# Half of the first k tile brought in uncast over SyncE's queue and cast on ScalarE, with new engine orders, in a fused attention and MLP kernel

## The chip, the cores and the metric

The kernel runs on one core of a Trainium2 chip. The metric is the device time of one execution in microseconds, the median of the runs shown. A profile of one execution of its own lies beside the runs.

## The reference

Two stages, the second of which eats what the first gives:

```
q, k, v: [8, 8, 576, 64]   beacon_k, beacon_v: [8, 8, 16, 64]      (batch, head, token, dim; float32)
k_all = concat(beacon_k, k);  v_all = concat(beacon_v, v)           592 keys
a = softmax(q k_all^T / 8), causal on the 576 tokens, the 16 beacon keys seen by all
x = (a v_all), heads side by side                                   [4608, 512]
h = x w_in;  g = h * sigmoid(1.702 h);  out = g w_out               [512, 2048], [2048, 512]
```

## The kernel before, in words

**Tiles and stages.** The 64 heads are worked in 16 sets of four (two sets to a batch). A set's q and k each come from HBM as one tile of 128 partitions by 1152 elements (18 tokens by 64 dims to a partition, `e_load_qk`, L415). The load is a DMA issued by POOL, and it casts float32 to float16 on its way. DVE turns each tile (`e_turn`, L464) by 32x32 transposes into `qT` and `kT`. TensorE makes the scores of a set in chunks (`e_qk`, L492): QK chunk 0 is the first half of the queries of set 0, chunk 1 that of set 1, chunks 2 to 4 the second half of set 0, chunks 5 to 7 that of set 1. ScalarE takes the exponentials (L517), DVE or POOL cuts them at the causal diagonal (L531, L538), TensorE multiplies by v (`e_av`, L597; with x = 2 it makes the softmax sums by a product with ones instead), DVE inverts the sums (`e_z1`, `e_z2`) and normalizes into `xT` (L631). From there the MLP runs in groups of tokens: group 0 is tokens 0 to 255, group 1 the next 256, later ones 512 tokens each. The first product is at L655 (`m1`), its gate in groups 0 and 1 is a tanh on ScalarE (L669) and a multiply on DVE (L688), the second product is at L700 and, for later groups, L769 (`m2`).

**PSUM.** Score chunks use one buffer `s` of four banks, so a new chunk waits until the exponential of the one before has read it. A ring of four more banks `u` serves everything else: AV products, m1 tiles, and the four heads of QK chunks 1 and 2 (`RINGED = (1, 2)`). A ring bank is free again when its reader is done: the exponential, the normalization, the z transpose, the gate.

**Order of the work.** The program makes a list of operations (`plan.op`) with what they depend on. Each gets a number in the order of its making. `ORDER` (L16) holds, written out for each engine, the numbers in the order in which that engine issues them. So each engine works strictly in that order, and an instruction that waits holds all behind it. DMAs issued by POOL (lists "POOL" and "Q") have eight in flight at most (`LANES`): the ninth issue waits on POOL until the first of them has landed. `lat` (L233) holds the delays with which the order was made.

**The start.** SP and ACT load the beacon keys of set 0 (`load_bk(0, 1, ...)`, four small DMAs), SP those of set 1 (four more). POOL issues q of set 0, k of set 0, k of set 1, q of set 1, then v and w_in in pieces: v of batch 0 in six (the beacon values and five blocks of keys, called v0 to v4 here), w_in in eight (four column quarters c0 to c3 by two row halves of 256 KB in float16 each). The orders of the first work, by names that stand for the numbers:

```
POOL q0 k0 k1 q1 | v0 w(c1) w(c0) v4 w(c0) beacon v, v2 v1 w(c2), keep masks, w(c1) | mask, q2 k3 v3 w(c2) ...
DVE  beacon cast, q0 turn, k0 turn, set 1's cast and two turns, masks, z and norms of the first halves,
     ..., three gates, ... k2 turn ...
PE   qk0 qk3 qk1 qk4 qk2 qk5 | AV sums of sets 0, 1; AV 1.1 | qk6 | AV 0.0, sums of set 0's second half,
     AV 0.1, AV 1.0 | qk7 | m1 (four of group 0), five AVs of the second halves, m1 (four), ...
ACT  exp 0, 0, 3, four of 1, 4, two of 2, 5, two of 2, 6, 7, then tanh
```

"AV 1.0" is the product of set 1 with the first of two interleaved halves of v. PE fills its early waits with dummy products on `scrap` (L1377), so that a busy PE before 16 us is not all work.

Of the kernel before, what the change touches and what calls it, by code (L numbers as in the profile page):

```python
# [8 lines left out]
F32 = mybir.dt.float32  # L9
# [8 lines left out]
        76, 119, 100, 101, 102, 103, 111, 122, 112, 113, 114, 140, 126, 149, 154, 142, 129, 133, 131, 152, 145, 163,  # L18
        166, 169, 172, 136, 138, 156, 161, 159, 175, 178, 184, 181, 199, 238, 205, 202, 217, 243, 208, 193, 245, 211,
        214, 248, 194, 220, 269, 187, 188, 223, 274, 195, 189, 276, 224, 196, 279, 190, 225, 411, 252, 283, 259, 255,  # L20
        226, 414, 229, 230, 231, 257, 417, 290, 288, 264, 262, 293, 286, 295, 424, 232, 323, 315, 311, 313, 301, 319,
        305, 307, 309, 303, 321, 317, 331, 327, 329, 325, 442, 433, 349, 354, 355, 350, 351, 356, 352, 445, 436, 440,
        438, 357, 360, 471, 376, 361, 362, 370, 363, 577, 371, 365, 372, 377, 366, 580, 481, 367, 373, 378, 368, 586,
        484, 379, 486, 488, 605, 382, 518, 496, 607, 383, 384, 385, 520, 610, 490, 512, 516, 492, 500, 494, 506, 502,
        514, 510, 504, 508, 498, 549, 543, 544, 538, 539, 540, 545, 541, 596, 738, 550, 565, 546, 551, 552, 741, 566,
        567, 568, 601, 744, 619, 599, 603, 554, 555, 751, 626, 624, 556, 557, 622, 769, 559, 560, 561, 562, 628, 772,
        760, 571, 572, 573, 648, 574, 658, 638, 656, 798, 765, 763, 654, 646, 632, 634, 642, 640, 644, 630, 650, 636,
        652, 808, 767, 703, 676, 677, 681, 682, 904, 683, 678, 704, 684, 679, 907, 705, 811, 815, 813, 913, 687, 688,
        697, 689, 690, 932, 706, 698, 692, 693, 699, 934, 694, 695, 700, 839, 937, 923, 709, 710, 711, 829, 821, 712,
        827, 837, 823, 817, 833, 835, 841, 819, 847, 825, 831, 843, 845, 1065, 946, 928, 865, 870, 866, 867, 871,  # L30
        868, 1068, 926, 930, 951, 949, 953, 1071, 876, 877, 878, 872, 873, 1078, 886, 887, 888, 879, 881, 882, 1096,
        883, 892, 893, 884, 894, 1099, 889, 961, 895, 1087, 1125, 898, 899, 900, 901, 969, 965, 957, 955, 967, 959,
        981, 963, 985, 979, 975, 973, 983, 977, 971, 1144, 1135, 1094, 1090, 1003, 1004, 1005, 1014, 1006, 1147,
        1140, 1092, 1142, 1138, 1153, 1008, 1009, 1015, 1019, 1016, 1010, 1172, 1011, 1017, 1020, 1203, 1021, 1174,
        1030, 1022, 1024, 1025, 1026, 1027, 1177, 1031, 1032, 1033, 1207, 1205, 1209, 1219, 1235, 1211, 1036, 1212,
        1037, 1215, 1038, 1039, 1239, 1237, 1163, 1186, 1251, 1223, 1221, 1241, 1243, 1244, 1253, 1225, 1255, 1247,
        1227, 1228, 1257, 1189, 1191, 1193, 1170, 1168, 1166, 1259, 1260, 1231, 1342, 1283, 1288, 1326, 1263, 1289,
        1284, 1328, 1330, 1358, 1290, 1285, 1286, 1360, 1344, 1291, 1362, 1346, 1332, 1294, 1334, 1335, 1295, 1348,
        1351, 1296, 1338, 1304, 1297, 1350, 1299, 1374, 1300, 1301, 1364, 1305, 1302, 1354, 1306, 1378, 1367, 1366,
        1380, 1307, 1382, 1383, 1376, 1310, 1311, 1312, 1316, 1313, 1370, 1386, 1317, 1318, 1319, 1449, 1465, 1406,  # L40
        1411, 1407, 1469, 1408, 1412, 1467, 1451, 1474, 1471, 1473, 1409, 1453, 1481, 1413, 1414, 1417, 1458, 1455,
        1418, 1457, 1427, 1419, 1477, 1420, 1487, 1485, 1483, 1497, 1422, 1423, 1428, 1424, 1490, 1425, 1461, 1489,
        1501, 1433, 1429, 1430, 1503, 1434, 1505, 1435, 1506, 1436, 1439, 1440, 1441, 1442, 1529, 1493, 1530, 1509,
        1499, 1531, 1534, 1550, 1540, 1551, 1532, 1541, 1535, 1542, 1536, 1537, 1552, 1553, 1543, 1545, 1546, 1547,
        1548, 1556, 1557, 1558, 1559, 1562, 1563, 1564, 1565,
    ],
    "ACT": [
        3, 1, 77, 79, 120, 107, 104, 105, 106, 123, 118, 117, 141, 116, 115, 143, 146, 164, 167, 170, 173, 176, 179,
        182, 185, 200, 239, 203, 206, 244, 209, 246, 212, 215, 249, 218, 270, 275, 277, 221, 280, 191, 197, 412, 415,
        227, 418, 425, 427, 233, 324, 314, 316, 302, 320, 308, 312, 306, 310, 322, 318, 304, 332, 328, 330, 326, 443,  # L50
        353, 446, 472, 475, 578, 581, 587, 590, 606, 608, 519, 521, 513, 491, 497, 517, 493, 495, 501, 515, 511, 503,
        507, 505, 509, 499, 611, 542, 739, 742, 745, 754, 752, 770, 773, 629, 649, 659, 639, 657, 799, 655, 635, 633,
        641, 643, 645, 647, 651, 631, 637, 653, 802, 905, 680, 908, 917, 914, 933, 935, 938, 840, 822, 828, 838, 818,
        824, 834, 836, 820, 848, 842, 826, 830, 832, 844, 846, 1066, 869, 1069, 1072, 1079, 1081, 1097, 1100, 1129,
        1126, 962, 966, 958, 970, 960, 956, 964, 968, 982, 986, 976, 974, 980, 984, 978, 972, 1145, 1007, 1148, 1157,
        1154, 1173, 1175, 1204, 1178, 1208, 1210, 1206, 1236, 1214, 1216, 1218, 1220, 1238, 1240, 1252, 1242, 1222,
        1224, 1226, 1254, 1246, 1250, 1248, 1230, 1258, 1256, 1234, 1232, 1343, 1266, 1327, 1264, 1262, 1359, 1329,
        1287, 1331, 1361, 1345, 1347, 1333, 1337, 1339, 1341, 1349, 1357, 1353, 1363, 1375, 1365, 1355, 1379, 1369,
        1373, 1377, 1381, 1385, 1387, 1371, 1389, 1450, 1466, 1470, 1452, 1472, 1468, 1410, 1454, 1476, 1480, 1456,
        1464, 1482, 1478, 1460, 1488, 1486, 1484, 1498, 1462, 1496, 1502, 1504, 1508, 1492, 1512, 1494, 1500, 1510,  # L60
        1533,
    ],
    "DVE": [
        73, 75, 74, 97, 98, 99, 80, 82, 81, 110, 109, 78, 108, 127, 128, 150, 151, 130, 132, 153, 155, 134, 92, 237,
        135, 165, 168, 171, 137, 87, 139, 157, 235, 158, 162, 174, 160, 177, 236, 180, 183, 186, 266, 267, 201, 207,
        204, 268, 210, 213, 216, 421, 408, 219, 409, 410, 222, 468, 297, 253, 254, 260, 423, 422, 261, 284, 256, 258,
        285, 291, 289, 265, 263, 292, 287, 294, 296, 300, 469, 470, 298, 299, 429, 430, 431, 337, 338, 341, 583, 333,
        334, 432, 342, 343, 335, 345, 434, 344, 339, 435, 336, 340, 346, 347, 437, 441, 439, 358, 348, 477, 585, 478,
        479, 480, 364, 584, 482, 483, 735, 369, 748, 485, 374, 487, 489, 380, 386, 750, 749, 737, 736, 615, 592, 522,
        523, 593, 534, 535, 536, 594, 795, 530, 526, 537, 531, 527, 528, 532, 595, 529, 533, 597, 598, 524, 525, 547,  # L70
        553, 616, 617, 618, 602, 620, 600, 621, 604, 627, 756, 625, 623, 757, 558, 758, 759, 563, 910, 569, 796, 761,
        797, 762, 575, 766, 764, 804, 912, 805, 911, 1075, 806, 807, 660, 661, 672, 668, 768, 809, 669, 662, 810,
        670, 673, 664, 663, 671, 665, 685, 674, 816, 812, 666, 667, 814, 919, 675, 920, 691, 921, 696, 922, 701, 924,
        1062, 707, 1077, 1063, 942, 925, 713, 1076, 1064, 943, 1195, 1150, 857, 944, 858, 849, 945, 1122, 850, 859,
        851, 947, 929, 853, 854, 948, 852, 861, 855, 862, 927, 931, 952, 856, 860, 954, 863, 864, 950, 1083, 874,
        1124, 1123, 1084, 1085, 880, 885, 1086, 890, 1196, 1088, 896, 902, 1131, 1089, 1152, 1132, 1133, 987, 988,
        989, 1151, 1197, 991, 992, 1134, 990, 1198, 1136, 999, 1095, 1137, 995, 996, 1000, 1091, 1141, 1093, 997,
        1139, 993, 1199, 1001, 1143, 998, 994, 1200, 1201, 1002, 1012, 1018, 1159, 1160, 1202, 1023, 1028, 1182,
        1161, 1034, 1162, 1213, 1183, 1217, 1184, 1185, 1040, 1267, 1164, 1165, 1268, 1187, 1245, 1249, 1188, 1229,
        1233, 1190, 1192, 1194, 1171, 1169, 1167, 1261, 1265, 1322, 1323, 1324, 1271, 1269, 1270, 1325, 1275, 1272,  # L80
# [42 lines left out]
class Plan:  # L123
# [109 lines left out]
    def lat(self, d, o):  # L233
        if o.eng == "Q":
            return 300 if d.eng == "SP" else 1200
        if d.name == "bk" and d.eng != "DVE":
            return {"bk0": 2500, "bk1": 5200}.get(o.name, 9000)
# [7 lines left out]
def kernel(  # L245
# [11 lines left out]
    nc = tc.nc  # L257
# [202 lines left out]
    def f32(ap):  # L460
        return ap.bitcast(F32)
# [952 lines left out]
```

## Time and profile before

| what | us |
|---|---|
| runs | 322.94, 323.44, 324.39 (median 323.44) |
| the profiled execution | 323.13 |
| its span | 321.4 |
| PE busy | 310.9 (97%) |
| DVE busy | 245.7 (76%) |
| ACT busy | 219.9 (68%) |
| POOL busy | 112.7 (35%) |
| QK chunk 0 starts on PE | 8.93 |
| first m1 matmul | 22.21 |
| last matmul ends | 317.6 |

The span is the time from the first to the last instruction of the program; 1.7 us of the execution lie around it. Busy shares are averages over the span. Where a row of the timeline gives "[idle before <-releaser]", it is the time the engine stood still ahead of this instruction and what ended the wait. The landing of a DMA is its issue time plus the microseconds that the DMA view gives it.

### The profile page before, as it was taken

The numbers are of one execution on the slowest core, as the hardware profiler recorded it, in microseconds if no ns is written. First come the engines' busy times: TensorE is split into PE (matmuls) and PEld (weight loads), VectorE is DVE, ScalarE is ACT, GpSimd is POOL, SyncE is SP. The second block draws the span as 40 slices with busy tenths as digits, with TensorE's granted clock in tenths as the row PEclk, the third lists the DMA queues.
The fourth block names the chain that finished last, engine by engine and source line by source line (L and its number), as shares of the span: only waits on it lengthen the run. The fifth ranks groups of instructions, "written<-read, shape, count | busy, mean of one in ns | idle before, by whom it ended". The sixth has DMA issues, their size and how long they took to land.

```text
span 321.4 us, 10238 instructions
## 1 busy us (share of the span) xinstructions
PE 310.9 (97%) x4465; PEld 230.0 (72%) x4465; DVE 245.7 (76%) x481; ACT 219.9 (68%) x277; POOL 112.7 (35%) x178
## 2 busy tenths in 40 slices
PE   7779999999999999999999999999999999999995
PEld 6557765644886467754778878746888888888884
DVE  3579963997894888976888969888988975684683
ACT  1783778686767787598867685778779786665520
POOL 7777558590226703573083208320320000000000
PEclk9999999999999999999999999999999999999999
DMA  7999999998028961299174707700021000010113
GB/s 120 159 194 206 195 198 179 197 188 104 2 63 115 168 91 35 20 163 122 23 78 88 120 4 71 107 33 2 4 72 61 2 20 17 33 68 34 68 58 107
DMA packets 58222, 28.85 MB, mean 90 GB/s; under 512 B 41280, under 2 KB 53568, under 8 KB 58176
## 3 DMA queue, kind: packets, MB, share of 16 engines
q0 software_dynamic: 47552, 18.49, 49.4%
q1 hardware_dynamic: 10560, 9.69, 9.2%
q8 instruction: 35, 0.57, 0.7%
q14 instruction: 11, 0.09, 0.1%
q10 hardware_dynamic: 64, 0.01, 0.0%
HBM read 37.22 MB, written 9.44 MB: 145 GB/s over the span
## 4 chain that ended last, share of the span: by engine, by line
PE 91%; DMA 3%; POOL 3%; ACT 1%; issue 1%; DVE 0%; POOLq 0%
PE u L769 31%; PE u L655 26%; PE u L856 11%; PE u L597 10%; PE s L506 8%; PE u L700 5%; DMA w<-in_moe_w_in_dram 3%; POOL w L439 1%; ACT E L517 1%; POOL vb L433 1%; POOL kn L417 0%; ACT L676 0%; POOL qn L417 0%; POOL E L538 0%; DVE xT L631 0%
## 5 line engine op out<-in xcount | busy, mean ns | idle before, releaser
L517 ACT ACTIVATE E<-s 128x2048 f16<-128x2048 f32 (+5 forms) x63 | 95.6, 1532 | 41.4 <-PE s L506 37.7
L655 PE MATMUL u<-xT,w 128*128 128x256 f16 (+1 forms) x512 | 87.4, 326 | 0.7 <-issue 0.5
L538 POOL TENSOR_SCALAR_AFFINE_SELECT E<-E 128x512 f16<-128x512 f16 (+3 forms) x78 | 48.1, 634 | 91.4 <-ACT E L517 91.3
L655 PEld LDWEIGHTS <-w 128*128 128x128 f16 x512 | 49.3, 98 | 33.7 <-issue 2.1
L676 ACT ACTIVATE g<-u 128x512 f16<-128x512 f32 x80 | 43.4, 600 | 15.7 <-PE u L655 15.2
L769 PEld LDWEIGHTS <-g 128*128 128x128 f16 x512 | 48.4, 98 | 6.9
L785 DVE SCALAR_TENSOR_TENSOR osb<-u,osb 128x512 f32<-128x512 f32 x48 | 32.9, 685 | 22.8 <-PE u L769 18.2
L769 PE MATMUL u<-w,g 128*128 128x256 f16 x384 | 50.2, 273 | 0.0
L769 PEld LDWEIGHTS <-sA 128*128 128x128 f16 x384 | 36.6, 98 | 4.9
L506 PEld LDWEIGHTS <-kT 32*128 32x128 f16 x1376 | 24.6, 92 | 19.7 <-issue 12.8
L884 ACT ACTIVATE g<-u 128x512 f16<-128x512 f32 x48 | 27.0, 602 | 15.0 <-PE u L856 9.1
L506 PE MATMUL s<-qT,kT 32*128 32x32 f16 (+20 forms) x1328 | 33.1, 228 | 2.4 <-ACT E L517 1.9
L769 PE MATMUL u<-tB,sA 128*128 128x256 f16 x256 | 34.2, 273 | 0.0
L631 DVE TENSOR_TENSOR xT<-u,rz 128x352 f16<-128x352 f32 (+2 forms) x52 | 26.1, 519 | 6.1 <-PE u L597 5.3
L433 POOL DMA_DIRECT2D vb<-in_v_dram x32 | 27.5, 861 | 3.8 <-DMA qn<-in_q_dram 1.5
L597 PE MATMUL u<-E,vb 128*32 128x352 f16 (+8 forms) x928 | 27.3, 262 | 0.7 <-DMA vb<-in_v_dram 0.4
L597 PEld LDWEIGHTS <-vb 128*32 128x32 f16 (+1 forms) x928 | 20.0, 96 | 6.1 <-issue 2.1
L556 DVE TENSOR_TENSOR zs<-zs,E 128x1344 f16<-128x1344 f16 (+2 forms) x36 | 21.6, 601 | 1.1
L473 DVE STREAM_TRANSPOSE qT<-qn 128x576 f32<-128x576 f32 x16 | 19.8, 1235 | 3.2 <-DMA qn<-in_q_dram 2.4
L473 DVE STREAM_TRANSPOSE kT<-kn 128x576 f32<-128x576 f32 x16 | 20.1, 1257 | 0.9 <-DMA kn<-in_k_dram 0.3
L856 PEld LDWEIGHTS <-w 128*128 128x128 f16 x192 | 18.7, 98 | 2.2
L856 PE MATMUL u<-xT,w 128*128 128x256 f16 x144 | 20.1, 273 | 0.0
(76 smaller groups left out, 388.2 us busy)
## 6 DMA issues: line engine op xcount, KB each, us to landing
out_dram<-osb SPq DMA_DIRECT2D x36, 256.0 KB, 2.3
qn<-in_q_dram POOLq DMA_DIRECT2D x16, 288.0 KB, 6.4
kn<-in_k_dram POOLq DMA_DIRECT2D x16, 288.0 KB, 6.2
vb<-in_v_dram POOLq DMA_DIRECT2D x24, 128.0 KB, 5.5
w<-in_moe_w_in_dram POOLq DMA_DIRECT2D x8, 256.0 KB, 9.4
w<-in_moe_w_out_dram POOLq DMA_DIRECT2D x4, 512.0 KB, 11.1
vb<-in_v_dram POOLq DMA_DIRECT2D x8, 112.0 KB, 5.9
vb<-in_v_dram POOLq DMA_DIRECT2D x8, 80.0 KB, 6.6
```

The costliest lines, as they stand in the source:

```text
L433: nc.gpsimd.dma_start(out=t[0 : hi - lo, j, h0:h1, :], in_=v[b, h0:h1, lo:hi, :].rearrange("h n d -> n h d"),)
L473: nc.vector.transpose(out=f32(dst.rearrange("p n e -> p (n e)")).rearrange("p (r t) -> p t r", t=TR), in_=f32(src[:, :]).rearrange("p (t c ...
L506: nc.tensor.matmul(ss[i][h][:, o : o + w], kT[s % NB2][r : r + 32, j * P : (j + 1) * P, d], qT[s % NB2][r : r + 32, a : a + w, d], start=( ...
L517: nc.scalar.activation(out=Es[s][:, :, c0:c1] if h is None else Es[s][:, h, c0:c1], in_=sall[i][:, :, o : o + c1 - c0] if h is None else s ...
L538: nc.gpsimd.affine_select(out=blk, in_=blk, compare_op=ALU.is_ge, fill=0.0, base=off + (Nb if j == 0 else 0), pattern=[[0, Q], [1, w]], ch ...
L597: nc.tensor.matmul(u[32 * h : 32 * h + 32, a:e], lhs, src[0:kw, h, col : col + e - a], start=first, stop=last, skip_group_check=s >= EARLY ...
L655: nc.tensor.matmul(u[:, o + a - t0 : o + e - t0], w1t[:, kp, nt * P : (nt + 1) * P], xT[:, kp, a % XR : (e - 1) % XR + 1], start=(kp == 0) ...
L676: nc.scalar.activation(out=gts[g][:, n0:n1, 0:w], in_=rings[("m1", g, n0)][:, 0 : n * w].rearrange("p (n w) -> p n w", n=n), func=AFT.Gelu ...
L769: nc.tensor.matmul(u[:, HM * mt : HM * (mt + 1)], lhs[:, n, mt * P : (mt + 1) * P], rhs[:, n, :], start=(n == 0 and mt == 0 and p not in ( ...
L785: nc.vector.scalar_tensor_tensor(out=osbs[(g, dst)][:, :], in0=rings[("p", g, p)][:, :], scalar=scale_of(g), in1=osbs[(g, src)][:, :], op0 ...
L856: nc.tensor.matmul(u[:, HM * n : HM * (n + 1)], lhs[x][:, (2 * i + n) * P : (2 * i + n + 1) * P], rhs[:, x, :], start=fresh and n == 0 and ...
L884: nc.scalar.activation(out=gts[g][:, n : n + 2, HM * h : HM * (h + 1)], in_=rings[src][:, :].rearrange("p (n w) -> p n w", n=2), func=AFT. ...
```

## The change

Half of set 0's k (the first 9 of the 18 tokens of each partition, 128x576 float32) is loaded uncast by SP into a stretch of `xT` that is not in use before batch 2, and ScalarE casts it into `kn[0]`. POOL loads only the other half. The DVE turn of this k is cut in two. The beacon keys of sets 0 and 1 come by four DMAs in place of eight, two each from SP and ACT, behind one memset in place of two.

```diff
+    HW = TR // 2 * D
+    staged = f32(xT[:, 0, XR - 2 * HW : XR])
+
+    def e_load_qk(s, which, part):
+        if part == 0:
+            nc.sync.dma_start(out=staged, in_=rows_of(k, 0)[:, 0:HW])
+            return
+        a = HW if part else 0
+        nc.gpsimd.dma_start(out=(qn, kn)[which][s % NB3][:, a:], in_=rows_of((q, k)[which], s)[:, a:])
+
+    def e_cast():
+        nc.scalar.mul(out=kn[0][:, 0:HW], in_=staged, mul=1.0)
...
-    def e_turn(s, which):
-        if which == 1:
+    def e_turn(s, which, part):
+        if which == 1 and part != 1:
...
+        t0, t1 = (0, TR) if part is None else (TR // 2 * part, TR // 2 * (part + 1))
...
-            out=f32(dst.rearrange("p n e -> p (n e)")).rearrange("p (r t) -> p t r", t=TR),
-            in_=f32(src[:, :]).rearrange("p (t c) -> p t c", t=TR),
+            out=f32(dst.rearrange("p n e -> p (n e)")).rearrange("p (r t) -> p t r", t=TR)[:, t0:t1, :],
+            in_=f32(src[:, :]).rearrange("p (t c) -> p t c", t=TR)[:, t0:t1, :],
...
-    load_bk(0, 1, (), ("SP", "ACT"))
-    load_bk(1, HS)
+    half = op("SP", 440, [], lambda: e_load_qk(0, 1, 0), pr=0, name="hl")
+    half = op("ACT", 680, [half], e_cast, pr=0, name="casta")
+    load_bk(0, HS, (), ("SP", "ACT"))
...
-    nc.vector.memset(bkf[:, 0:1, :], 0.0)
-    nc.vector.memset(bkf[:, 1:HS, :], 0.0)
+    nc.vector.memset(bkf[:, 0:HS, :], 0.0)
...
+        if d.name == "hl":
+            return 2300
         if d.name == "bk" and d.eng != "DVE":
-            return {"bk0": 2500, "bk1": 5200}.get(o.name, 9000)
+            return {"bk0": 2500, "bk1": 2500}.get(o.name, 9000)
```

`ORDER` is replaced as a whole. Chunks 1 and 2 are in ring banks in both kernels. The same operations stand in the new lists, but for those above. At the start they read:

```
SP   half of k0, beacon keys, beacon keys
ACT  beacon keys x2, cast, exp 0, 0, four of 1, 3, two of 2, 4, two of 2, 5, 6, tanh, 7, then tanh
POOL other half of k0, q0 k1 q1 | w(c1) w(c1), keep masks, v1 v0, beacon v, q2 v2 v4 v3 w(c0) w(c0)
     w(c2) w(c2) | three masks, k2 w(c3) w(c3) ...
DVE  beacon cast, k0 turn in two halves, q0 turn, set 1's cast and two turns, masks, z and norms,
     ..., q2 turn, ..., casts of sets 3 and 2, four gates, ... k2 turn ...
PE   qk0 qk1 qk3 qk2 qk4 | AV sums of set 0, AV 0.1, AV sums of set 1 | qk5 | AV 1.1, AV 0.0, AV 1.0, sums
     of set 0's second half | qk6 | m1 (two of group 0) | qk7 | m1 (three), five AVs, m1 (three), qk8, ...
```

In PE's list the changes between the three kinds of products (scores, AV, MLP) number 126 in both kernels. ACT's list changes between the exponential's and the gelu's table 13 times before and 15 times after; the added pair puts the exponential of QK chunk 41 between the gelus of group 5. From the last products of the list backwards, the same product ends it, and the same chain of join and store follows.

## The prediction

> **What bounds the kernel now.** I read the table by stage first: each row is a stretch of the span, then the busy time of the engines in it.
>
> ```profile
> core 0: us, PE busy (x) PEld busy (x) DVE busy (x) ACT busy (x) POOL busy (x), PEclk, DMA share, GB/s
> 2.40:8.90 6.50, 6.04 (x18) 4.55 (x17) 2.75 (x5) 0.84 (x1) 5.36 (x9) 1.00 1.03 175
> 8.90:22.20 13.30, 9.77 (x315) 7.61 (x315) 7.87 (x20) 11.02 (x14) 10.91 (x20) 1.00 1.45 173
> 22.20:25.20 3.00, 2.41 (x35) 1.70 (x20) 2.89 (x7) 2.54 (x3) 1.00 (x2) 1.00 1.53 192
> 25.20:60.00 34.80, 34.80 (x564) 22.95 (x565) 25.56 (x48) 24.52 (x27) 22.40 (x36) 1.00 1.42 196
> 60.00:317.60 257.60, 257.47 (x3552) 192.85 (x3549) 204.98 (x396) 180.54 (x233) 71.70 (x108) 1.00 0.42 68
> ```
>
> From 25.2 us to the last matmul PE stands still for 0.13 us in all. What is left to gain lies before: PE's busy time there is partly dummies (3.08 us of the 9.77 by the rows of L1377), the DMA share is 1 or more, and ACT is busy 11.0 of 13.3. So the price of any edit is how much sooner or later PE gets its work in the first 35 us; after that the time follows one for one. Next the timeline of that stretch:
>
> ```profile
> 7.61 1.26 DVE L473 STREAM_TRANSPOSE kT<-kn 128x576 f32<-128x576 f32 x1 [0.26 <-DMA kn<-in_k_dram]
> 8.93 0.31 PE L506 MATMUL s<-qT,kT 32*128 32x288 f16 x4 [0.49 <-DVE kT L473]
> 12.24 1.45 ACT L517 ACTIVATE E<-s 128x1536 f16<-128x1536 f32 x1 [0.66 <-PE s L506]
> 20.04 1.45 ACT L517 ACTIVATE E<-s 128x1536 f16<-128x1536 f32 x1 [0.17 <-PE s L506]
> ...
> 19.21 0.28 PE L597 MATMUL u<-E,vb 128*32 128x176 f16 x8 [0.39 <-DMA vb<-in_v_dram]
> 21.64 1.19 DVE L631 TENSOR_TENSOR xT<-u,rz 128x288 f16<-128x288 f32 x3 [0.82 <-PE u L597]
> 22.21 2.47 PE L655 MATMUL u<-xT,w 128*128 128x256 f16 x18
> 25.18 1.70 PE L655 MATMUL u<-xT,w 128*128 128x256 f16 x14 [0.50 <-issue]
> 25.34 2.02 DVE L688 SCALAR_TENSOR_TENSOR g<-sig,u 128x512 f16<-128x512 f16 x3
> ```
>
> The reader is to see: the first scores wait for k's landing, the AV products for a block of v, the m1 products for the norms, and the m1 ring for DVE's gates. Last the DMA view, one issue at a time. Issue plus its time to landing gives: q0 6.0, k0 7.5, k1 9.0, q1 10.4, v0 11.2, w(c1) 13.0, w(c0) 14.9, v4 15.5, w(c0) 16.8, beacon v 17.0, v2 18.5, v1 19.2. POOL's queue is a line: 1.5 us a q or k tile, 0.5 to 0.7 a v block (v2 1.5), 1.3 for most w quarters, but 1.8 and 1.9 for the first two. The packets show why: while those two move, the queue gives 132 GB/s, against 204 around 19 us.
>
> **First scores.** Removed: half of k0 from POOL's line, 0.75 us. The first full tile landed at 6.0, so the half lands at 5.3, q0 at 6.8. Added: 295 KB by SP. No row shows such a load; the nearest are the 256 KB stores by SP, 2.13 to 2.2 us from issue to landing when quiet, and the 4 KB beacon loads, 1.5 when issued at 1.03 but 4.3 when issued at 1.94 behind POOL's packets. SP issues before POOL's data flows (2.4), so I take the store: landed near 3.2. Its own time on the engines is bounded by 0.9 us (q1 row: 9.69 MB in 9.2% of the span, 0.33 MB/us) and by nothing, if it all falls into the idle time ahead of 2.4; I take 0.1 as POOL's delay, since most of it falls there: q0 at 6.9. The cast (ACT, 576 columns, near the 0.60 of 512) waits for the SP load, behind it only the exponentials, which need the scores anyway. Three fewer DMAs are issued by SP; the two beacon loads behind the big one on SP cost nothing if they land before 5. DVE turns both halves of k0 (0.65 each, half of 1.26, and 0.2 for the beacons) before 6.9. Then q0's turn replaces k0's as the last step: 8.93 less 7.5 is 1.4 from landing to scores, so 8.3 in place of 8.93, **0.6 us sooner**.
>
> **Exponentials.** The new order puts the four of chunk 1 second. They need q1, which lands at 9.8 (6.9 + 1.5 + 1.4); turned by 11.2, scores 11.25, exponential 0.65 later, 11.9. ACT resumed at 12.24 before. So **0.3 of the 0.6 is left**; q1 is late next. From start to start the rows give 1.9 for four, 1.35 for a 1536-wide one, 0.85 for a pair: 11.9 + 1.9 + 1.35 + 0.85 + 1.35 + 0.85 = 18.2 for chunk 5.
>
> **The wait that the new PE order adds.** AV 0.1 now stands ahead of qk5 and needs v2, the last of its blocks. In the new POOL line v2 follows 0.75 less of k, one w quarter less (1.3), no v4 (0.5), but q2 (1.5): 19.2 - 0.75 - 1.3 - 0.5 + 1.5 + 0.1 = **18.2**. The two w(c1) loads are the first touches of both row halves, so I let them keep the slow 1.8 and 1.9. Behind AV 0.1 on PE wait the sums of set 1 (0.3) and qk5, and for qk5 ACT: chunk 5 starts 19.3, not 18.2. Chunk 6's scores stand behind the sums of set 0's second half, which wait for a ring bank (norm, 20.5): qk6 21.05, its exponential 21.65 to 23.1, where before it ended at 21.5. The norms gain though: set 1's sums end 18.65, z transpose, reciprocal and transpose (0.48, 0.22, 0.48 and hops) to 20.0, four norms to 21.65, where before they ended at 22.83. First m1 at 21.8 needs w(c1), landed by 13.7, the next w(c0), 18.2 + 1.0 + 2.6 = 21.8, in time. The three masks now behind all of that on POOL start near 16.9 (v0 and the beacon v free POOL's eight in flight at 15.7) and end by 18.9, before their product.
>
> **The ring.** An m1 tile costs PE 0.87. Two tiles to 23.5, qk7 to 24.05, two more to 25.75; before, the same four and qk7 ended at 26.88. So PE is 1.1 ahead here. But exponential 7 now comes between the first tanh (24.15) and the second (25.6 to 26.2). DVE reaches its gates at 25.1 (norms 21.65, then z 0.5, memsets 0.65, q2's turn 1.25, rest of z 0.65, two casts 0.4), the first ends 25.8, the second must wait and ends 27.0, then 0.65 each. PE: fifth tile 25.85 to 26.7, AVs at 27.1, 27.75, 28.4, 28.9, 29.5 as gates and norms free banks, tiles at 30.0, 31.15, 32.0, qk8 33.0 (k2's turn ends 32.95), first tile of group 1 33.55 to 34.4. Before, the same work ended at 34.69. PE stands for about 1.2 us between 26.7 and 32, and is **0.3 ahead** at the end of it.
>
> **The rest.** Same products, same 126 changes of kind, same last product and store. Two table changes more on ACT, 1.28 each, are hidden by ACT's slack (180.5 of 257.6) and by six products and qk41 beside them; without that cover they cost up to 2.6. Sum: 323.13 of the profiled execution (span 321.4 + 1.7) less 0.3 is **322.8**. The median of the runs lies 0.31 above the profiled one; on it the same sum reads 323.1. I give 322.8.
>
> **Rivals.** (a) *V comes early.* If w(c1) moves at 1.3 twice, v2 lands at 17.0, AV 0.1 hardly waits, and 1.2 us of the loss at qk5 is not there; with half of the ring's standing gone, 322.8 - 1.2 - 0.6 = **321.0**. For it: later w quarters all take 1.3. Against: both slow ones were the first. (b) *The AV wait grows: slower.* AV 0.1 holds PE, qk5 and ACT one for one with v2's landing. If the SP load costs POOL's line its full 0.9, and a w or v2 load loses 0.6 more, v2 lands at 19.7 and m1 starts 1.5 later; with the ring wait of 26.7 to 32 0.9 longer, because exponential 7 holds the second tanh, 322.8 + 1.5 + 0.9 = **325.2**. It turns the result from gain to loss when v2 lands after 18.5. For it: v2 took 1.5 before, twice v1. Against: less data stands ahead of it. (c) *The early load is hidden.* The SP load only takes its bytes out of POOL's share: q0 lands at 7.5 as k0 did, everything is 0.6 later, **323.4**. Against: before 2.4 us the engines are idle (share 0.02). [...]
>
> **How the numbers follow.** 322.8 has 0.45, (a) 0.26, (b) 0.20, (c) 0.09. A measurement of this kernel can tell about 0.5%, 1.6 us, from no change: faster below 321.8, slower above 325.1. Tails of the forecast's own steps (each landing is good to 0.3, the ring to 0.5) add little. Range 320.9 to 325.2. Faster 0.28, same 0.51, slower 0.21.
>
> **What would show it.** Right: first scores at 8.3, four exponentials of chunk 1 from 11.9, AV products waiting on vb until about 18.2, m1 at 21.8, PE idle near 1.2 us between 26 and 32, none after 35. Wrong: w(c1) landing 1.3 us apart, v2 before 17.5 or after 19, q0 after 7.3, PE idle beyond 35 us, or ACT's added table pair with PE idle beside it near 180 us.

## The result, and the profile of the changed kernel

| | us |
|---|---|
| changed kernel, median of 19 runs | 325.72 (323.53 to 327.79) |
| kernel before, median of 19 runs beside them | 323.4 (322.59 to 324.87) |
| ratio | 1.0075, 95% interval 1.0059 to 1.0091 |
| profiled execution of the changed kernel, its span | 324.70, 323.0 |

Forecast were 322.8 and a range up to 325.2. The change costs 2.3 us where 0.3 were to be gained. The ratios here leave disturbed executions out of both kernels, so that some lie nearer to one than the quotient of the medians beside them.

First the table by stage of the changed kernel, cut as before (busy time of each engine in the stretch; the last product ends 1.3 us later).

```profile
core 0: us, PE busy (x) PEld busy (x) DVE busy (x) ACT busy (x) POOL busy (x), PEclk, DMA share, GB/s
2.40:8.90 6.50, 4.45 (x19) 3.40 (x22) 3.03 (x7) 1.60 (x2) 6.34 (x13) 1.00 1.04 183
8.90:22.20 13.30, 11.11 (x294) 8.38 (x294) 8.97 (x22) 10.33 (x14) 9.93 (x15) 1.00 1.54 171
22.20:25.20 3.00, 1.71 (x44) 1.40 (x42) 2.81 (x8) 2.54 (x3) 1.94 (x4) 1.00 1.19 209
25.20:60.00 34.80, 34.36 (x548) 22.75 (x551) 26.47 (x44) 23.89 (x29) 23.97 (x36) 1.00 1.39 190
60.00:318.90 258.90, 258.38 (x3576) 193.94 (x3568) 204.72 (x394) 184.44 (x235) 71.54 (x107) 1.00 0.43 68
```

PE is busier from 8.9 to 22.2 (11.11 us for 9.77) and stands still for much of the next 3 us (busy for 1.71 of 3.00). After 25.2 it stands for 0.44 + 0.52 us where it stood for 0.13. Ahead of 8.9 it is busy for 4.45 in place of 6.04: the fillers end at 6.8 us, and the scores start at 8.8. The timeline of the start shows why:

```profile
3.72 0.68 ACT L430 ACTIVATE kn<-xT 128x576 f16<-128x576 f32 x1 [0.40 <-DMA xT<-in_k_dram]
7.51 1.26 DVE L484 STREAM_TRANSPOSE qT<-qn 128x576 f32<-128x576 f32 x1 [0.47 <-DMA qn<-in_q_dram]
8.82 0.64 PE L517 MATMUL s<-qT,kT 32*128 32x288 f16 x24 [2.05 <-DVE bkn L471]
```

The half of k is there at 3.7 and cast at 4.4, but q lands at 7.5, as the whole k did before, and its turn is the last step. (The wait is put down to the cast of `bkn` that follows the turn on DVE.) PE's timeline of 18 to 32 us then shows where it stands still:

```profile
18.20 0.21 PE L608 MATMUL u<-E,vb 128*32 128x48 f16 x4 [0.22 <-DMA vb<-in_v_dram]
...
21.52 1.91 PE L666 MATMUL u<-xT,w 128*128 128x256 f16 x16
23.36 0.54 PE L517 MATMUL s<-qT,kT 32*128 32x208 f16 x32
25.36 2.78 PE L666 MATMUL u<-xT,w 128*128 128x256 f16 x24 [1.46 <-issue]
...
31.56 2.34 PE L666 MATMUL u<-xT,w 128*128 128x256 f16 x20 [0.28 <-issue]
```

The first m1 product starts at 21.52, 0.7 sooner than before. Then PE stands for 1.46 us, "<-issue": nothing that the profile shows held it. In the program the m1 tile behind it waits for no semaphore at all. The page's part on the DMA queues names a candidate, beside the count of PE's instructions:

```profile
PE 310.4 (96%) x4466; PEld 230.2 (71%) x4466; DVE 247.7 (77%) x481; ACT 223.2 (69%) x280; POOL 115.0 (36%) x178
q8 instruction: 35, 0.57, 0.8%
```

The queue "instruction" moved 0.57 MB in 35 packets, 16 KB each. PE's matmuls and weight loads number 8932, which is 255 to a packet.

To compare the kernels, I add up the time that the products streamed so far would take back to back (without fillers; products on a quarter of the array count a quarter). The changed kernel is 0.2 us ahead of the one before at 24 us; it is behind by 0.6 at 34 us, 0.5 at 120, 1.1 at 140 and 1.2 at 280.

### The profile page after: what moved, and what is told of

Read it like the earlier page. It is cut to its first block, busy times and chain, and to the rows that moved or that the text cites. A ratio compares the mean times of both kernels' runs of the same rounds, so it can differ in the third digit from the quotient of the medians.

```text
span 323.0 us, 10237 instructions
## 1 busy us (share of the span) xinstructions
PE 310.4 (96%) x4466; PEld 230.2 (71%) x4466; DVE 247.7 (77%) x481; ACT 223.2 (69%) x280; POOL 115.0 (36%) x178
## 4 chain that ended last, share of the span: by engine, by line
PE 92%; DMA 5%; issue 1%; DVE 1%; POOL 0%; POOLq 0%
PE u L780 31%; PE u L666 26%; PE u L867 11%; PE u L608 10%; PE s L517 9%; PE u L711 5%; DMA vb<-in_v_dram 3%; DMA kn<-in_k_dram 2%; DVE osb L796 1%; POOL kn L427 0%; POOL qn L427 0%; POOLq L1416 0%
## 5 line engine op out<-in xcount | busy, mean ns | idle before, releaser
L549 POOL TENSOR_SCALAR_AFFINE_SELECT E<-E 128x512 f16<-128x512 f16 (+3 forms) x78 | 50.3, 663 | 95.6 <-ACT E L528 90.3
L780 PE MATMUL u<-tB,sA 128*128 128x256 f16 x256 | 35.7, 273 | 0.0
L877 ACT ACTIVATE u<-u 128x512 f32<-128x512 f32 x24 | 14.1, 591 | 9.8 <-PE u L867 8.8
L484 DVE STREAM_TRANSPOSE kT<-kn 128x576 f32<-128x576 f32 (+1 forms) x17 | 20.1, 1194 | 0.7
```

Source lines behind the costliest of these rows:

```text
L484: nc.vector.transpose(out=f32(dst.rearrange("p n e -> p (n e)")).rearrange("p (r t) -> p t r", t=TR)[:, t0:t1, :], in_=f32(src[:, :]).rear ...
L549: nc.gpsimd.affine_select(out=blk, in_=blk, compare_op=ALU.is_ge, fill=0.0, base=off + (Nb if j == 0 else 0), pattern=[[0, Q], [1, w]], ch ...
L780: nc.tensor.matmul(u[:, HM * mt : HM * (mt + 1)], lhs[:, n, mt * P : (mt + 1) * P], rhs[:, n, :], start=(n == 0 and mt == 0 and p not in ( ...
```

## The experiments

Three theories came out of this, and the experiments use their letters. **T**: TensorE's own instructions come in batches of 256 (8932 in 35 packets are 255 to one); while the loads are moving, the next batch is there about 5.8 us after the one before (5.7 to 6.2 in the changed kernel's profile), and PE, which now gets its work sooner, only waits for it. **C**: since fewer fillers stand ahead of the scores, TensorE's clock falls in many executions (a mean granted clock under .997 in 12 of 19). **D**: with the early half on SyncE's queue, q lands late in some executions (at 6.83 to 9.14 us in ten profiles). **S** is the view that the early half alone costs the time, **R** that the number of instructions does not matter and the new order itself is what costs. "Below .997" counts the runs whose mean granted clock was under that: one spell of 3.41 us at half speed takes 0.005 off the mean, and in the 16 profiles a spell that began only after the last product took at most 0.003.

| kernel | median us | ratio to before, interval | runs below .997 |
|---|---|---|---|
| e1 early half, old orders | 325.1 | 1.0041 (1.0015 to 1.0068) | 9 of 12 |
| e2 new orders, no early half | 324.76 | 1.0046 (1.003 to 1.0062) | 2 of 7 |
| e3 changed, +106 instructions | 328.59 | 1.0149 (1.0111 to 1.0187) | 6 of 6 |
| e4 changed, +234 instructions | 328.5 | 1.0165 (1.0141 to 1.0188) | 4 of 4 |
| e5 changed, wide fillers | 325.37 | 1.0043 (1.0016 to 1.007) | 9 of 12 |
| e6 e5 and 28 units of fillers | 325.87 | 1.0067 (1.0043 to 1.0091) | 5 of 12 |
| e7 before, wide fillers | 323.9 | 1.0007 (0.9991 to 1.0023) | 9 of 12 |
| e8 changed, fillers split | 329.23 | 1.0172 (1.0139 to 1.0205) | 4 of 4 |
| e9 e2 with wide fillers | 323.87 | 1.0011 (0.9992 to 1.003) | 4 of 12 |
| e10 e5 and 12 units of fillers | 324.15 | 1.0019 (1.0001 to 1.0037) | 2 of 12 |
| e11 e1, wide fillers, 12 units more | 323.74 | 1.0007 (0.9986 to 1.0028) | 4 of 12 |
| e12 before, 18 units fewer | 324.94 | 1.0039 (1.0023 to 1.0054) | 5 of 11 |
| e13 e9 and 12 units of fillers | 323.77 | 1.002 (1.0009 to 1.0031) | 3 of 12 |
| e14 changed, 12 units more | 326.17 | 1.0088 (1.0074 to 1.0103) | 0 of 6 |

The kernel before ran beside them at 323.14 (e1 to e4), 323.51 (e5 to e8), 323.42 (e9 to e12) and 323.21 (e13, e14). Its own runs below .997 were 5 of 18, 12 of 29, 17 of 34 and 5 of 17; their median over all four groups is 323.73, that of the others 323.14. So a low mean clock is no mark of the changed kernel alone, and in the kernel before it went with 0.6 us.

**The two halves of the change.** e1 keeps the early load, cast and split turn and puts the old `ORDER` back (with the half of k ahead of q on POOL). e2 keeps the new `ORDER` and brings all of k by POOL:

```diff
-            nc.sync.dma_start(out=staged, in_=rows_of(k, 0)[:, 0:HW])
             return
-        a = HW if part else 0
+        a = 0
...
-        nc.scalar.mul(out=kn[0][:, 0:HW], in_=staged, mul=1.0)
+        pass
```

> The early half of k0 (SP load, cast on ACT, split turn, k0 ahead of q0 on POOL) with the order of before for all else. Theory T (PE waits for its own instructions: in both profiles PE stood still just ahead of its records 449, 705, 961, 256 apart, each time until about 2.2 us after an instruction-queue packet of 16384 bytes started, and the new order reaches them sooner and so waits longer): the order of before meets these places late, so the time is that of before, 323.4 within 0.7, with one wait near record 705 of 0.5 to 1 us. Rival S (the early half itself costs: its bytes push POOL's line and the norms): at least 1.5 us above before, 325 or more.

> The new order with the whole of k0 loaded by POOL and no load on SP and no cast. Theory T: the loss belongs to the order, so the time is that of after, 325.7 within 1, with the waits near records 449, 705 and 961 (0.4, 1.3 to 1.6, 0.3 to 0.6 us). Rival S: the loss goes with the early half, and this one is at or below before, 323.4 within 0.7.

Neither T nor S was borne out as they stood (T missed e1, S missed e2): each half costs about 0.4% by itself. e2 has the stalls, 0.68 us at 25.4 and 0.28 at 31.6 in PE's timeline, both "<-issue", and few runs below .997. e1 runs at a lower clock in 9 of 12; its three other runs have a median of 322.98. But e1's profile (326.58) has a stall of the same kind too, in the middle of 32 like products:

```profile
24.83 2.58 PE L667 MATMUL u<-xT,w 128*128 128x256 f16 x19
28.50 1.59 PE L667 MATMUL u<-xT,w 128*128 128x256 f16 x13 [1.09 <-issue]
```

**More instructions.** e3 and e4 replace the fillers between qk0 and qk1 by 64 or 128 tiny products on a corner of the array:

```diff
+                if o.name == "open1":
+                    for y in range(64):
+                        r = 32 * (y % 4)
+                        nc.tensor.matmul(
+                            idle[r : r + 32, 0:64], scrap[:, 0:32], scrap[:, 0:64], start=True, stop=True
+                        )
+                    n = 0
```

> After, with the dummy products between the first two score chunks (8 float32 and 3 float16 ones) replaced by 64 very small float16 ones of about the same time: some 106 more records on PE ahead of all later work, and nothing else changed. Theory T: the waits stay at records 449, 705 and 961 of PE's own count and so fall about 106 records earlier in the work: none at the third m1 tile near 24 us, one of 0.7 to 1.5 us near 28 to 29 among the AV products; time 0.3 to 1 us under after, 325. Rival R (the ring banks, gates and tanh hold the third m1 tile): the wait of 1.5 us stays at the third m1 tile, time as after.

> The same with 128 small dummies, some 234 more records than after. They end before q1 is turned, so PE has the room. Theory T: record 449 now falls on the scores near 14.6 us, whose instructions can't be there before about 16; a new wait of 1 to 2 us there, exponentials later by 1 us, another near 20; time 1 to 2.5 us above after, 327 to 328. Rival R: nothing that waits for data has changed; time as after within 0.5.

Both were slower than expected, and at a clock of .984 in the profile: in e3's PE is busy for 0.25 us of the 3.4 from 6.8 and for 1.77 of the next 3.4, tiny products included, and from 13.6 to 17.0 the clock is at half. So the time does not tell T from C. The place of the stalls does. Counting PE's and PEld's instructions in the order of their start, the first one after each long stall is as follows (the expectations count three or four higher: 449, 705, 961):

| kernel | instruction number | stall, start to start, us | packet of "instruction" starts | stall ends |
|---|---|---|---|---|
| before | 702 | 0.77 | 22.89 | 25.18 |
| changed | 446, 701, 957 | 0.46, 1.53, 0.55 | 17.29, 23.14, 29.28 | 19.49, 25.36, 31.56 |
| e1 | 702 | 1.36 | 26.25 | 28.49 |
| e4 | 447, 702, 957, 1213 | 1.64, 0.51, 2.05, 1.03 | 15.87, 22.05, 29.45, 35.99 | 18.36, 24.39, 31.67, 38.41 |
| e3 | 702, 2236 | 1.49, 3.26 | 22.24, 67.30 | 24.47, 69.74 |

Within a kernel they come at multiples of 256 from each other, give or take two, whatever the instruction is (a score, an AV product or an m1 product), and end 2.2 to 2.5 us after a packet starts; e4, with 9166 instructions, has 36 packets for 35.

**The same TensorE time in fewer or more instructions.** e5 makes each filler twice as wide (40 filler instructions for 68: the changed kernel's 11 fillers in 32 bit left 22 matmuls and 22 weight loads in the trace, so that one counts four, and the 12 in 16 bit left 12 and 12, so that one counts two); e8 turns each 32-bit filler into four 16-bit ones (112). e6 is e5 with 28 more units (of 256 columns) ahead of the scores; e7 is the kernel before with wide fillers.

```diff
-                for x in [f32(scrap)] * (n // 4) + [scrap] * (n % 4):
-                    nc.tensor.matmul(idle[:, 0:COLS], x[:, 0:P], x[:, 0:COLS], start=True, stop=True)
+                todo = [(f32(scrap), 2)] * (n // 8) + [(f32(scrap), 1)] * (n % 8 // 4)
+                todo += [(scrap, 2)] * (n % 4 // 2) + [(scrap, 1)] * (n % 2)
+                for x, r in todo:
+                    y = x[:, 0:COLS].rearrange("p (o c) -> p o c", o=1).to_broadcast([P, r, COLS])
+                    nc.tensor.matmul(idle[:, 0 : r * COLS], x[:, 0:P], y, start=True, stop=True)
```

> The changed kernel with its filler matmuls made twice as wide (the same TensorE time, 40 filler instructions instead of 68; nothing else changed). Theory T (in 13 to 32 us TensorE is held by the supply of its own instructions, 256 at a time, each batch some 5.8 us after the first instruction of the batch before): 28 instructions fewer ahead of the batches that were waited for, at 5.85 us / 256 = 23 ns each, so 0.6 us less than the changed kernel, 325.1 against 325.7, with the stalls near records 702 and 957 shorter or with more useful work done when they come. Rival R (the order of the work itself costs the time, its waits and bank handovers): no change against the changed kernel, 325.7 +-0.3. Theory C (clock falls in spells after the idle stretch at 6.8 to 8.8 us) is left as it is: granted clocks of .992 to 1.0 as before.

> The changed kernel with each 32-bit filler split into four 16-bit ones of the same total time (112 filler instructions instead of 68). Theory T: 44 instructions more at 23 ns, 1.0 us more than the changed kernel, 326.7; the stalls again come at the same record numbers (near 446, 702, 957), that is, earlier in the useful work. Rival R: as the changed kernel, 325.7 +-0.4.

> As the run with wide fillers, and 3 wide and one single filler more ahead of the first scores (3.0 us of TensorE time in the program's count of 28 units, 16 instructions), so that TensorE is busy in 6.8 to 8.8 us. Theory C: the granted clock is 1.0 in all or nearly all runs and the time falls by the share of runs that were slow times their cost, some 0.8 us, to 324.3 (324.9 if the 16 instructions cost their 0.4 us by theory T). Without C: clocks between .992 and 1.0 as in the changed kernel, and 325.1 to 325.7. If the fillers run past 8.8 us, the first scores come later by that.

> The kernel before with its filler matmuls made twice as wide (36 filler instructions instead of 66). Theory T: the stalls of 0.77 us at 25.2 and 0.25 us at 30.4 go down by up to 30 x 23 ns = 0.7 us, less what data is late anyway: 322.7 (322.4 to 323.0) against 323.2. Rival R: 323.2 +-0.2.

e8 is 3.5 us slower than the changed kernel, not 1.0, and its stalls are again near 446, 701 and 957. A late one is the largest; PE's timeline shows that it splits one chunk's 24 like products into 18 and 6:

```profile
66.83 0.60 PE L517 MATMUL s<-qT,kT 32*128 32x384 f16 x18
70.44 0.26 PE L517 MATMUL s<-qT,kT 32*128 32x48 f16 x6 [3.00 <-issue]
```

PE is busy for 0.69 us in the window of 3.41 us with this stall, and the clock is at half in the next one (PEclk is the third column from the right):

```profile
66.75:70.16 3.41, 0.69 (x30) 0.35 (x18) 3.31 (x7) 0.00 (x0) 3.20 (x4) 1.00 1.27 219
70.16:73.58 3.42, 3.14 (x13) 1.15 (x14) 3.15 (x5) 2.83 (x4) 2.93 (x5) 0.50 2.03 142
73.58:76.99 3.41, 3.41 (x17) 1.57 (x16) 2.10 (x2) 1.88 (x3) 2.55 (x4) 1.00 1.18 148
```

The clock is back after one such window. In e5's profile (322.65, clock 1.0) the stall of 1.46 us is all but gone (0.35 from start to start at instruction 701, for 1.53); the same two groups follow each other, and the stretch from 22.2 to 25.2 is full:

```profile
23.11 0.54 PE L517 MATMUL s<-qT,kT 32*128 32x208 f16 x32
23.59 3.04 PE L666 MATMUL u<-xT,w 128*128 128x256 f16 x24
```

```profile
22.20:25.20 3.00, 3.00 (x55) 2.46 (x54) 2.57 (x7) 2.54 (x4) 1.72 (x3) 1.00 1.19 209
```

Instruction 961 starts at 31.78 in both, but by then e5 has streamed 1.49 us more of products. So 28 instructions fewer gave 1.49 us of work, 53 ns each; that is about 14 m1 products with their weight loads, at the 109 ns from one m1 product to the next in the changed kernel's trace. My 23 ns (5.85 us by 256) were too low, since each instruction that drops out makes room for work that is worth more. The median moved by 0.35 only, and 9 of 12 runs were below .997: T alone is not all. e6 failed as a trial of C: the fillers ran to 11.06 us where scores could have started near 10, and its 325.87 says nothing for or against. e7 missed: no gain in the median, 323.03 in the three runs above .997. The kernel before had less to win: the 0.25 us at 30.4 that I had counted as a stall is at instruction 947 and was ended by a norm on DVE, so only the 0.77 us at 702 was of this kind, and in e7 a stall of 0.70 us at instruction 446 (20.2 us) stands in its place. Why 9 of 12 of e7's runs were below .997, for 12 of 29 of the kernel before beside it, is open.

**The clock.** e10 adds 12 units to e5 ahead of the scores, e11 gives e1 the same fillers, and e9 gives e2 the wide ones. e12 takes 18 units away from the kernel before, and writes the rest as 16-bit products, so that the number of instructions stays (62 for 66):

```diff
+                if o.name == "qk0":
+                    n -= 18
+                wide = [] if o.name == "qk0" else [f32(scrap)] * (n // 4)
+                for x in wide + [scrap] * (n - 4 * len(wide)):
```

> The new orders alone (the whole of the first k by GpSimd's queue, no early half) with the wide fillers: 40 filler instructions instead of 68. Theory T (instruction supply): 28 x 23 ns = 0.6 us less than the orders alone, 324.1 against 324.8, and 1.5 us more useful work done at record 961. Theory D (the early half of k on SyncE's queue makes q's first load land anywhere between 7.0 and 8.9 us, and the late ones bring the idle TensorE and the lower clock): without it q lands near 7.0 and the times of the single runs lie within some 1.5 us of each other, with few of them below a clock of .997, where the changed kernel with wide fillers ran from 322.65 to 326.89. Against D: the same scatter as that kernel.

> The changed kernel with wide fillers, and 12 units (1.3 us at full clock) of them more ahead of the first scores, so that they end at 7.6 to 8.9 us. Theory C (the clock falls for 3.41 us after each free-running window of 3.41 us in which the array streamed for less than about 0.35 of its area times time; without these fillers the window over 5.2 to 10.2 us is near 0.34): fewer runs below .997 than the 9 in 12 of the kernel with wide fillers alone, and a median of 323.7 (323.0 to 324.5) instead of 325.4. Theory D alone (late loads decide): as that kernel, 325.4 +-0.5.

> The early half with the orders of before (325.1), with wide fillers (44 instructions for 64) and 12 units more of them ahead of the first scores. T and C together: 323.3 (322.6 to 324.5), most runs at a clock above .997. D alone: 324.5 to 325.5, as the early half alone, since q lands late in some runs.

> The kernel before with 18 units (1.9 us at full clock) fewer of fillers ahead of the first scores, the rest of them as 16-bit matmuls so that the number of instructions stays (62 for 66). Loads, orders and all work as before. Theory C: the window over 6 to 9 us is nearly empty, the clock falls to half for 3.4 us in most runs (.989 to .995), and the time goes up by some 1 us, 324.5 (323.8 to 326). Against C: 323.4 +-0.3, as before, since these fillers wait for nothing and nobody waits for them.

e10 has 2 of 12 runs below .997 for e5's 9, and its median is 1.2 us lower although it has 8 instructions more. e12 is 1.5 slower than before, with fillers taken away that nobody waits for. What happened is not the fall that I expected but a late rise. PE's timeline of e12, then that of before:

```profile
2.03 3.59 PE L1380 MATMUL u<-tB 128*128 128x256 f16 x16 [2.03 <-DVE tB L328]
8.88 1.04 PE L506 MATMUL s<-qT,kT 32*128 32x288 f16 x24 [3.26 <-DVE kT L473]
9.85 4.00 PE L1380 MATMUL u<-tB 128*128 128x256 f32 x9
```

```profile
2.03 6.41 PE L1377 MATMUL u<-tB 128*128 128x256 f32 x18 [2.03 <-DVE tB L328]
8.93 0.64 PE L506 MATMUL s<-qT,kT 32*128 32x288 f16 x24 [0.49 <-DVE kT L473]
9.50 2.10 PE L1377 MATMUL u<-tB 128*128 128x256 f32 x9
```

The same nine fillers take 4.00 us for 2.10, the same 24 scores 1.04 for 0.64. In the trace's clock records full clock begins at 14.9 us in e12, at 7.1 in before. The mean clock does not show it: e12's profile reads .998. e9 came out as T said (324.1 expected, 323.87; 0.9 less than e2), with stalls that are small: 0.25 and 0.13. e11's 323.74 lies in the range of T and C together.

**What is left.** e13 is e9 with e10's fillers, thus e10 without the early half; e14 is the changed kernel with its narrow fillers and 12 units more.

```diff
+            if o.name == "qk0":
+                n += 12
```

> The new orders without the early half, with the same fillers as the changed kernel with wide fillers and 12 units more (324.15). Theory D0 (with the clock and the instruction supply made equal, the early half of k is worth nothing, since q lands at 6.9 to 7.1 us with it or without it): 324.1 +-0.4. Rival: the early half still gains its 0.3 to 0.6 us here: 324.5 to 324.8. Theory D (the early half makes q late in some runs): a smaller scatter and 323.7.

> The changed kernel with its own narrow fillers and 12 units more of them ahead of the first scores (80 filler instructions for 68). Theory C: far fewer runs below a clock of .997 than the 12 in 19 of the changed kernel, which by itself takes the median from 325.7 towards the 324.9 of that kernel's undisturbed runs; theory T: the 12 instructions more cost 12 x 23 ns = 0.3 us. Together 325.2 (324.6 to 325.6). Without C: 326.0.

e13 is not slower than e10: with equal fillers the early half is worth nothing. In e14 no run is below .997, yet it is not faster than the changed kernel, and 1.2 us slower than the seven runs of that kernel that were not below .997 either (324.93, below). PE's timeline has the stalls in the middle of a chunk of 24 and one of 32 like products:

```profile
19.36 0.51 PE L517 MATMUL s<-qT,kT 32*128 32x288 f16 x19
21.03 0.21 PE L517 MATMUL s<-qT,kT 32*128 32x32 f16 x5 [1.17 <-issue]
...
25.11 0.51 PE L517 MATMUL s<-qT,kT 32*128 32x208 f16 x26
27.11 0.22 PE L517 MATMUL s<-qT,kT 32*128 32x32 f16 x6 [1.49 <-issue]
```

So the clock's share was not to be had by narrow fillers; the gain of full clock and the cost of the 12 instructions came out at no gain. The time is not T's alone, since q landed at 8.63 in this profile and the scores began 1.1 us later than in the changed kernel's; the place of the stalls is. No version beats the kernel before: e11 and e7 come nearest, at 1.0007.

## Why the prediction was wrong, point by point

**First scores: failed.** Forecast were the half of k at 3.2, q at 6.9, scores at 8.3; it was 3.70, 7.48 and 8.82, so 0.1 of the 0.6 was gained. The term that was mis-sized is POOL's delay, put at 0.1: q landed 0.7 after the 6.8 that the forecast had without a delay (POOL's half of k at 5.59 for 5.3). The forecast let most of the early load fall ahead of 2.4 us; SyncE's queue moved 0.12 of its 0.31 MB by then and the rest up to 4. POOL's own packets moved 0.10 MB in the microsecond from 3 to 4 and 0.17 from 4 to 5, where the kernel before moved 0.16 in each. Rival (c) had this step right (q at 7.5): q landed at 7.48 behind the same bytes as k before, at 7.52, so with half of k on SyncE's queue the last of these bytes came no sooner. Rival (c) worked out 323.4 from this step; the profiled execution took 324.70, so the other 1.3 us lie in the steps below. Nor is 7.48 fixed: in the ten profiles with the early half q lands at 6.83 to 9.14, in six of them after 7.9; in the three of the new orders without it (e2, e9, e13) at 6.98, 6.87 and 7.45. That it is the early half which scatters it (D) rests on these few profiles and is not settled: e13's runs scatter less than e10's (323.33 to 325.21 for 322.99 to 325.67), though only a little.

**Exponentials.** Chunk 1's were to start at 11.9 and started at 12.47: q of set 1 landed at 10.39 and not at 9.8, for the same delay.

**The AV wait: right.** v2 landed at 18.16 (18.2), the AV product waited until 18.20, m1 started at 21.52 (21.8). The second w(c1) landed at 13.8 (13.7). Rival (a) had its sign, w(c1) 1.3 apart (12.51, 13.83), but v2 was no sooner for it. Rival (b) did not happen: v2 was not after 18.5, and its 325.2 is near the result by luck, for a reason that it does not name.

**The ring: the step that failed.** I had PE stand 1.2 us between 26.7 and 32 for banks and gates, and 0.3 ahead at 34.4. It stood 1.46 us before 25.36 and 0.28 before 31.56, for its next instructions, and was 0.6 behind. The row of before was in my own fence, 0.50 "<-issue" at 25.18, and I read it as the ring. It was the same wait: instruction 702. An order that has its work ready sooner meets that wait sooner: in the changed kernel batches began at 13.76, 19.49 and 25.36, and the next ones at 19.49, 25.36 and 31.56, so 5.7, 5.9 and 6.2 us later. The sum had no term for TensorE's instructions at all. What e5 gained with 28 instructions fewer shows that this bound, not a bank or a gate, set the end of the stage.

**The fillers: the step that was missing.** They were counted as PE's busy time that is not work, and their number at nothing. The changed kernel has 15 passes of them ahead of the scores for 18, since the planner expected q sooner. Its profile has the clock at .999, so the 324.70 does not show what they cost; the runs do. Twelve of 19 were below .997, with a median of 326.68, against 324.93 for the other seven. So the median lies 1.0 above the profiled execution, where the forecast had 0.31 for that of before. The 1.75 us between the two sorts of runs are not the clock's alone: a late load (e1, scores at 10.28 us) or a stall (e8, 3.00 us) costs time by itself and was followed by half clock (10.58 to 13.99 in e1, 70.16 to 73.58 in e8), and the runs do not part the two.

**The rest.** "None after 35" was wrong by 0.36 us at 131, "<-issue" again, at instruction 4026, and by some lead lost elsewhere. The two added table loads were hidden, as forecast: from 170 to 182 us PE stood for 0.08 us at most.

**Shares.** Of the 2.3 us, wide fillers and 12 units more give back 1.6 (325.72 to 324.15), by T and C together. For T stand 0.9 (e2 to e9) and the 1.49 us of work at instruction 961; for C 1.2 (e5 to e10). They cannot be added up, since half clock followed a stall too (3.42 us of it in e8). What is left, 0.5 to 0.7 (e13, e10), is open. It is not shown to be the new order's own: e10's profile still has stalls at 446, 701 and 957 (0.55, 0.83 and 0.48 us from start to start), and e9, the same order, came to 1.0011 (0.9992 to 1.003). That each batch is asked for near the start of the one before is inferred from the times, and that the load on the DMA engines makes it late is my estimate from the starts of the packets (below): no run here took the load away.

## What to carry to other kernels

Where an engine stands still "<-issue" and the program has no wait there, count its instructions: stalls 256 instructions apart, in the middle of like products, pointed here to its instruction supply, and fewer, larger instructions ahead of that point were worth more (0.9 us from e2 to e9) than an earlier operand (nothing from e13 to e10). Fillers were neither free nor idle here: with 12 units more of them 2 of 12 runs were below .997 for 9 of 12 (e10, e5), and with 28 instructions fewer PE had streamed 1.49 us more at instruction 961 (e5), so here they had best be few, wide and as long as the wait. And read the clocks of all runs, those of the kernel before too, and not the profiled one's alone.

## What the runs showed of the hardware

**Instruction supply.** In the changed kernel a batch of 256 PE instructions that PE waited for began 5.7 to 6.2 us after the batch before, with a DMA share of 1.85, 1.21 and 1.23 between the two; its packet started 3.5 to 3.9 us after that batch had begun. In e4 one took 7.3 us, with its packet after 5.1. In before, the packet started after 0.4 where the DMA share was 0.00 (126.67 to 127.10 us); from 84 us on it started between 2.5 us ahead of the batch and 1.3 us behind.

**The clock.** Spells of lower clock last 3.41 us (e8) or twice that (e3, 6.8 us between 10.2 and 20.4), at half speed: the 32-bit matmuls of the fillers of before follow each other at 0.427 us ahead of 7.1 us, where its record of full clock begins, and at 0.216 behind it. For each window of 3.41 us between clock records in the first 80 us of the 16 profiles I took the columns streamed, times the share of the array that they use, over what the window could hold at full clock (32 times 256 columns, at a quarter of those 0.427 us each; a 32-bit matmul counts twice its columns). A product counts in the window in which it starts. At full clock, the ten windows after which it fell had 0.08 to 0.34; the lowest after which it did not had 0.34, 0.34, 0.35 and 0.38. The changed kernel's window from 5.2 to 8.6 us, with fillers up to 6.8 and nothing behind them, is one of those at 0.34. In e8 half clock lasts from 8.72 to 12.13 us and again from 70.16 to 73.58, 18 such windows later; the changed kernel's full clock begins at 5.2 us, that of before at 7.1. So a window with a third of the array's work was followed by a fall in one profile and by none in another, and one window of e11 with 0.55 of its time covered by products, 0.33 by area, was followed by a fall.
